# Token groups of 4, 8, 8, 8, 8, 8, 8 and 4 blocks in place of 6 and 8 in turn

## The chip, the cores and the metric

The kernel runs on one core of a Trainium2 chip. The metric is the device time of one execution in microseconds, the median of several runs. The core has a matrix engine (TensorE, PE in the profile, with its weight loads as PEld), VectorE (DVE), ScalarE (ACT), GpSimd (POOL) and SyncE (SP); POOL and SP also issue most of the transfers, each in the order of its own queue.

## What is computed

Attention with squared ReLU instead of softmax, for 8 batches of 12 heads, 448 positions and 64 columns each, and then a two-layer network over the 3584 tokens, with a sigmoid-approximated gelu between the layers:

```python
scores = scale * np.matmul(q, k.transpose(0, 1, 3, 2))
attn = np.maximum(scores, 0.0) ** 2 / S
attn_out = np.matmul(attn, v)
x = attn_out.transpose(0, 2, 1, 3).reshape(3584, 768)
h = x @ w_in                                # 768 -> 2048
g = h * (1.0 / (1.0 + np.exp(-1.702 * h)))
out = g @ w_out                             # 2048 -> 768
```

## The kernel before

**Attention.** The work is cut into 24 units: unit u is batch u // 3 and four of its twelve heads. A unit has 7 slots (key blocks of 64). For each slot four 64x64 score matmuls run side by side on TensorE (`scores`, L145), ACT or VectorE takes the ReLU out of PSUM (`relu2`, L159 and L156), VectorE squares (L430), and after the seventh slot 28 matmuls with v (`av_mm`, L174) give the unit's result, which `xt_evac` (L194, L197) copies to `xt`, the input of the first layer. The q and k of units 0 to 5 are loaded by POOL with a cast to 16 bits and transposed on TensorE (L129, L133); those of later units are loaded by SP (L82), cast by ACT (k) and POOL (q), and transposed by a transfer of SP (L111).

**Tokens.** A block is 64 tokens; 7 blocks make a batch, 56 the whole. The network works on groups of blocks, `gblk` (L41): 6, 8, 6, 8 and so on. A group's first layer needs all units that have a block of it. Two blocks are one tile of 128 tokens.

**First layer** (`m1`, L222): for each of 16 column blocks of `w_in`, six matmuls as wide as the group has tokens (384 or 512) into one of two PSUM banks (`ps_m`), then the gelu on ACT (L227, out buffer `gf`) and a scaling on POOL into `gt` (L229), the input of the second layer.

**Second layer.** Group 0 is done plainly (`m2`, L248): 2 x 16 matmuls of 384 columns for each tile. From group 1 on, two neighbouring tiles are done together by Strassen's scheme (`pair`, L287): seven products of 8 matmuls, 56 in place of 64, with sums of activations on VectorE (L282), sums of weights made once (`weight_sum`, L272, in quarters, called A to E), and evictions by ACT (L296) and VectorE (L298). A group of 6 blocks has three tiles: one pair, and one tile that has no partner (`single`), with two half products of 16 matmuls, 32 in all.

**Order.** The order of all instructions is written out as a string of words, and each engine takes its own part of it in that order. Words are: `s2.1` score slot 1 of unit 2 with its ReLU (`:d` on VectorE, `:t` scores issued twice, `:h` ReLU held back until after the next gelu or product), `x2.1` its square, `a2` the unit's matmuls with v and their copy to xt (`:m` in the two `ps_m` banks), `f0.3` column block 3 of group 0 in the first layer, `m` a plain half tile, `p1.0.4` product 4 of the pair that starts at tile 0 of group 1, `i` half a single. `jk`, `jq`, `jv` are POOL's loads of a unit's k, q, v, `jw` one of four blocks of w_in in two halves, `jo` one of four blocks of w_out; `k3` and `q3` are TensorE's transpositions; `G` a small copy that holds SP back until a block of w_out is there; `L`, `K`, `Q`, `R`, `W` loads, casts, transposition and v of later units; `z3` three matmuls of 512 zero columns into the buffer of the next scores. POOL's loads use eight semaphores in turn, so that each waits for the eighth before it.

Of the kernel before, what the change touches and what calls it, by code (L numbers as in the profile page):

```python
# [8 lines left out]
F32 = mybir.dt.float32  # L9
F16 = mybir.dt.float16  # L10
AF = mybir.ActivationFunctionType
ALU = mybir.AluOpType
# [3 lines left out]
def kernel(  # L16
# [9 lines left out]
    nc = tc.nc  # L26
    B, H, S, D = q.shape
# [10 lines left out]
    WO = 8  # L38


    gblk = [6, 8] * (B // 2)  # L41
    gcum = [0]
    for n in gblk:
        gcum.append(gcum[-1] + n)
# [14 lines left out]
    ps_s = ctx.enter_context(tc.tile_pool(name="ps_s", bufs=3, space=bass.MemoryType.PSUM))  # L59
    ps_m = ctx.enter_context(tc.tile_pool(name="ps_m", bufs=2, space=bass.MemoryType.PSUM))  # L60
# [74 lines left out]

    early = []

    def scores(u, j, times=1):
        st = units[u]
        sc = early.pop() if early else ps_s.tile([128, 2, 512], F32, name="sc", tag="sc")  # L140
        for s in [0, 1] * times:
            for a in range(2):
                r = slice(64 * a, 64 * a + 64)
                c = slice(64 * s, 64 * s + 64)
                nc.tensor.matmul(  # L145
                    out=sc[c, a, 0:S],
                    lhsT=st["kT"][r, j, c],
                    rhs=st["qT"][r, :, c],
                    start=True, stop=True)
        return sc  # L150

    def relu2(u, j, sc, dve=False):
        rl = rlp.tile([128, 2, S], F16, name="rl", tag="rl")
        at = atp.tile([128, 2, S], F16, name="at", tag="at")
        if dve:
            nc.vector.tensor_scalar(out=rl, in0=sc[:, :, 0:S], scalar1=0.0, scalar2=None,  # L156
                                    op0=ALU.max)
        else:
            nc.scalar.activation(out=rl, in_=sc[:, :, 0:S], func=AF.Relu)  # L159
        pend[u, j] = (at, rl)  # L160
        return at

# [43 lines left out]
    def release():  # L206
        while held:
            u, j, sc = held.pop()
            ats[u, j] = relu2(u, j, sc)
# [187 lines left out]
    with tc.manual_schedule():  # L397
# [21 lines left out]
                   "D": (w_d, wout[1][0], wout[0][0], ALU.add)}  # L419

        def slot(how, u, j):
            sc = scores(u, j, 2 if "t" in how else 1)
            if "h" in how:
                held.append((u, j, sc))
            else:
                ats[u, j] = relu2(u, j, sc, "d" in how)
# [13 lines left out]
        def zeros(how, n):  # L440
            early.append(ps_s.tile([128, 2, 512], F32, name="sc", tag="sc"))
            for _ in range(n):
                nc.tensor.matmul(out=early[0][:, 0, :], lhsT=zero[:, 0:128],
                                 rhs=zero[:, 0:512], start=True, stop=True)

        do = {"s": slot, "x": square, "z": zeros,
              "k": lambda how, u: trans_pe(u, "k"), "q": lambda how, u: trans_pe(u, "q"),
              "a": av,
# [20 lines left out]
            "f1.0 C0 m0.1.0 f1.1 K7 m0.0.0 s6.0:d s6.1 Q7 L8 s6.2 x6.0 A3 f1.2 f1.3 f1.4 f1.5 "
            "x6.2 s6.3 s6.4:h x6.1 E0 Q8 s6.5:d x6.3 x6.5 W6 R7 jo1.0 f1.6 A1 f1.7 s6.6 C3 s7.0 "  # L470
            "f1.8 x6.6 x6.4 K8 x7.0 f1.9 f1.10 L9 s7.1 Q9 R8 a6 L10 W7 s7.2 s7.3 E3 A2 f1.11 "
            "x7.1 C1 x7.2 K9 R9 x7.3 f1.12 s7.4:h s7.5 x7.5 m0.0.1 B3 B0 s7.6 B1 x7.6 x7.4 K10 "
            "Q10 s8.0 s8.1 x8.0 x8.1 f1.13 m0.1.1 A0 s8.2 x8.2 W8 a7 s8.3:d s8.4 L11 B2 m0.2.1 "
            "s8.5 x8.4 x8.3 s8.6 f1.14 D3 x8.5 x8.6 f1.15 W9 s9.0:d s9.1 x9.0 a8 R10 L12 s9.2 "
            "s9.3 p1.0.0 K11 f2.0 f2.1 C2 f2.2 x9.2 f2.3 x9.1 s9.4 s9.5:h x9.3 s9.6 p1.0.1 f2.4 "
            "D1 f2.5 f2.6 x9.4 E2 f2.7 s10.0 Q11 L13 x9.6 K12 s10.1:h s10.2:h x9.5 x10.0 f2.8 "
            "p1.0.2 x10.1 p1.0.3 Q12 x10.2 s10.3 a9 E1 x10.3 s10.4:d s10.5 f2.9 W10 f2.10 f2.11 "
            "R11 f2.12 p1.0.4 R12 x10.4 x10.5 s10.6 x10.6 s11.0 D0 s11.1 D2 f2.13 x11.0 W11 "
            "x11.1 p1.0.5 s11.2 a10 L14 s11.3:h s11.4 p1.0.6 x11.4 x11.2 Q13 K13 p1.2.0 f2.14 "
            "s11.5 x11.3 s11.6 f2.15 x11.5 p1.2.1 x11.6 L15 p1.2.2 s12.0 a11 s12.1 x12.0 "  # L480
            "s12.2:h p1.2.3 Q14 p1.2.4 s12.3 R13 x12.1 K15 s12.4:h K14 s12.5 x12.2 p1.2.5 "
            "p1.2.6 f3.0 f3.1 x12.5 x12.4 x12.3 s12.6:h s13.0:h s13.1 Q15 i2.2.1 R14 x13.1 "
            "i2.2.0 x13.0 L16 W12 p2.0.0 p2.0.1 s13.2:h L17 x12.6 a12 s13.3 f3.2 R15 f3.3 W13 "
            "x13.2 x13.3 f3.4 f3.5 p2.0.2 f3.6 s13.4 Q16 s13.5 s13.6 x13.4 f3.7 x13.5 W14 x13.6 "
            "f3.8 s14.0:d Q17 s14.1 x14.1 s14.2:h x14.0 K16 f3.9 W15 L18 p2.0.3 f3.10 x14.2 a13 "
            "s14.3 s14.4 f3.11 f3.12 x14.4 K18 x14.3 f3.13 K17 R16 f3.14 s14.5 s14.6 R17 "
            "s15.0:d x14.5 p2.0.4 x15.0 p2.0.5 x14.6 W16 W17 f3.15 s15.1:d a14 x15.1 s15.2:h "
            "s15.3 x15.3 p2.0.6 f4.0 s15.4:d x15.2 s15.5 s15.6:h p3.0.0 f4.1 f4.2 f4.3 x15.4 "
            "x15.5 Q18 L19 L20 x15.6 f4.4 s16.0:h s16.1:d s16.2 p3.0.1 x16.1 p3.0.2 x16.2 "
            "p3.0.3 K19 a15 s16.3:h s16.4 p3.0.4 p3.0.5 x16.0 R18 x16.4 p3.0.6 f4.5 Q19 W18 "  # L490
            "s16.5 s16.6 x16.5 s17.0:h x16.3 f4.6 p3.2.0 f4.7 x16.6 s17.1 s17.2:d x17.2 R19 "
            "x17.0 a16 x17.1 f4.8 p3.2.1 f4.9 p3.2.2 p3.2.3 f4.10 s17.3 s17.4 s17.5 p3.2.4 "
            "f4.11 x17.4 s17.6:h x17.3 W19 s18.0 x17.5 p3.2.5 x17.6 x18.0 p3.2.6 f4.12 L21 Q20 "
            "s18.1 K20 a17 s18.2 s18.3:h x18.1 f4.13 f4.14 L22 x18.2 f4.15 s18.4:d x18.4 "
            "s18.5:h f5.0 i4.2.1 Q21 x18.3 s18.6 x18.5 W20 s19.0:d x19.0 s19.1 x18.6 R20 i4.2.0 "
            "f5.1 f5.2 x19.1 p4.0.0 s19.2 a18 Q22 s19.3:h s19.4 f5.3 f5.4 K22 f5.5 p4.0.1 K21 "
            "x19.2 x19.3 f5.6 x19.4 f5.7 p4.0.2 s19.5 s19.6 L23 s20.0 p4.0.3 f5.8 x19.5 x19.6 "
            "f5.9 p4.0.4 Q23 x20.0 s20.1 s20.2 R21 x20.1 x20.2 a19 s20.3:h s20.4 f5.10 p4.0.5 "
            "p4.0.6 K23 x20.3 s20.5 x20.4 s20.6 s21.0 f5.11 x20.5 x20.6 R22 f5.12 s21.1:d s21.2 "
            "x21.1 x21.0 a20 s21.3:d s21.4 f5.13 x21.4 x21.2 x21.3 f5.14 f5.15 p5.0.0 s21.5 W21 "  # L500
            "x21.5 s21.6 s22.0:h f6.0 x21.6 p5.0.1 f6.1 p5.0.2 p5.0.3 x22.0 s22.1 a21 s22.2 "
            "s22.3 x22.3 f6.2 f6.3 x22.2 R23 f6.4 f6.5 p5.0.4 f6.6 x22.1 W22 f6.7 s22.4 s22.5:d "
            "s22.6 x22.5 p5.0.5 p5.0.6 p5.2.0 x22.6 f6.8 x22.4 s23.0:d x23.0 s23.1:h p5.2.1 "
            "p5.2.2 s23.2 s23.3 x23.1 a22 x23.2 s23.4 f6.9 f6.10 W23 f6.11 f6.12 x23.3 f6.13 "
# [40 lines left out]
```

## Time and profile before

| | |
|---|---|
| median of 5 runs | 382.64 us (382.53 to 384.86) |
| the profiled execution | 383.17 us, of which the span from first to last instruction is 381.4 us |
| granted clock of TensorE | 0.998 |
| first layer, matmuls of 512 columns | 384, 379 ns each from issue to end |
| first layer, matmuls of 384 columns | 384, 326 ns each from issue to end |
| ReLU on ACT | 144, 917 ns |
| square on VectorE | 168, 664 ns |
| gelu on ACT, 512 and 384 columns | 64 each, 599 and 493 ns |

Matmuls overlap: the time from one start to the next is shorter than the duration in the table. The page's second part cuts the span into 40 slices of 9.5 us; a digit is the busy share in tenths:

```profile
PE   7789999999999999999999999999999999999994
DVE  3999763778958886556788875638777865313374
ACT  2887763796776758367664656476764461232210
POOL 7555552753254323056340424332142231222200
DMA  8999999799946595789872809541730423101133
```

TensorE is full from the fourth slice to the last but one; VectorE and the DMA engines are full in the first slices; ACT, VectorE and POOL are lightly loaded in the last six, where attention is over.

### The profile page before, as it was taken

How to read it: one execution, taken by the hardware profiler on the slowest of the kernel's cores; microseconds unless marked ns; L12 is line 12 of the kernel's file. 1: busy time of each engine (PE TensorE's matmuls, PEld its weight loads, DVE VectorE, ACT ScalarE, POOL GpSimd, SP SyncE). 2: the span in 40 equal slices, each digit the busy share in tenths (PEclk: the TensorE clock that was granted, in tenths of full speed). 3: DMA queues.
4: the chain of work that ended last, by engine and by line, in shares of the span. 5: the costliest groups of instructions: out<-in, count | busy, mean ns of one | idle time of the engine just before them, and what ended most of it. 6: DMA issues, size and time to landing. Idle time of an engine off the chain costs nothing.

```text
span 381.4 us, 7864 instructions
## 1 busy us (share of the span) xinstructions
PE 369.5 (97%) x3136; PEld 192.8 (51%) x3136; DVE 256.6 (67%) x425; ACT 214.6 (56%) x314; POOL 136.2 (36%) x200
## 2 busy tenths in 40 slices
PE   7789999999999999999999999999999999999994
PEld 3355555445455555544555555544455555455552
DVE  3999763778958886556788875638777865313374
ACT  2887763796776758367664656476764461232210
POOL 7555552753254323056340424332142231222200
PEclk9999999999999999999999999999999999999999
DMA  8999999799946595789872809541730423101133
GB/s 120 169 190 205 205 265 220 149 193 185 252 143 144 87 288 132 189 143 177 143 209 76 168 7 300 109 128 22 142 62 0 108 26 83 43 0 41 43 83 83
DMA packets 65221, 50.85 MB, mean 133 GB/s; under 512 B 35744, under 2 KB 61728, under 8 KB 65184
## 3 DMA queue, kind: packets, MB, share of 16 engines
q1 hardware_dynamic: 47872, 35.70, 38.7%
q0 software_dynamic: 17152, 14.55, 26.4%
q8 instruction: 24, 0.39, 0.4%
q10 hardware_dynamic: 160, 0.10, 0.1%
q14 instruction: 13, 0.11, 0.1%
HBM read 45.61 MB, written 11.01 MB: 148 GB/s over the span
## 4 chain that ended last, share of the span: by engine, by line
PE 89%; DVE 5%; DMA 3%; issue 2%; ACT 1%; POOL 0%; ACTq 0%; POOLq 0%
PE ht L222 39%; PE op L287 29%; PE sc L145 9%; PE av L174 7%; PE op L248 4%; DMA k<-in_k_dram 3%; DVE at L430 2%; DVE osb L298 1%; PE tr L129 1%; DVE xt L197 1%; DVE kT L133 0%; DVE qT L133 0%; ACT eb L296 0%; ACT rl L159 0%; DVE as L282 0%
## 5 line engine op out<-in xcount | busy, mean ns | idle before, releaser
L222 PE MATMUL ht<-xt,win 128*128 128x384 f16 (+1 forms) x768 | 156.2, 353 | 0.4 <-ACT gf L227 0.4
L229 POOL TENSOR_SCALAR gt<-gf 128x384 f16<-128x384 f32 (+1 forms) x128 | 82.5, 645 | 200.2 <-ACT gf L227 197.8
L159 ACT ACTIVATE rl<-sc 128x896 f16<-128x896 f32 x144 | 126.2, 917 | 42.9 <-PE sc L145 35.5
L227 ACT ACTIVATE gf<-ht 128x384 f32<-128x384 f32 (+1 forms) x128 | 69.6, 546 | 85.3 <-PE ht L222 75.8
L430 DVE TENSOR_TENSOR at<-rl 128x896 f16<-128x896 f16 x168 | 105.9, 664 | 13.6 <-ACT rl L159 13.0
L222 PEld LDWEIGHTS <-win 128*128 128x128 f16 x768 | 72.4, 98 | 74.9 <-issue 12.0
L287 PEld LDWEIGHTS <-gt 128*128 128x128 f16 x408 | 38.6, 98 | 30.1 <-issue 3.8
L145 PE MATMUL sc<-qT,kT 64*64 64x448 f16 x696 | 48.6, 357 | 1.1 <-ACT rl L159 0.7
L287 PEld LDWEIGHTS <-as 128*128 128x128 f16 x312 | 29.9, 98 | 22.9 <-issue 2.9
L287 PE MATMUL op<-wsum,gt 128*128 128x384 f16 x224 | 40.6, 326 | 0.0
L287 PE MATMUL op<-wout,as 128*128 128x384 f16 x224 | 40.0, 326 | 0.0
L298 DVE SCALAR_TENSOR_TENSOR osb<-op,osb 128x384 f32<-128x384 f32 (+1 forms) x45 | 23.6, 544 | 23.6 <-PE op L287 23.3
L156 DVE TENSOR_SCALAR rl<-sc 128x896 f16<-128x896 f32 x24 | 26.1, 1087 | 16.2 <-PE sc L145 15.8
L174 PE MATMUL av<-at,v 64*64 64x448 f16 x616 | 33.2, 350 | 0.2 <-DVE at L430 0.2
L287 PE MATMUL op<-wout,gt 128*128 128x384 f16 (+1 forms) x184 | 32.4, 319 | 0.5 <-DVE osb L298 0.5
L194 DVE CAST xt<-av 128x896 f16<-128x896 f32 (+2 forms) x32 | 24.5, 792 | 11.6 <-PE av L174 11.6
L298 DVE SCALAR_TENSOR_TENSOR osb<-op,ea 128x384 f32<-128x384 f32 x22 | 12.1, 552 | 27.8 <-PE op L287 12.2
L145 PEld LDWEIGHTS <-kT 64*64 64x64 f16 x696 | 17.2, 105 | 24.8 <-issue 17.2
L174 PEld LDWEIGHTS <-v 64*64 64x64 f16 x672 | 19.7, 107 | 12.8 <-issue 2.7
L282 DVE TENSOR_TENSOR as<-gt 128x1024 f16<-128x1024 f16 x36 | 24.5, 706 | 0.7 <-POOL gt L229 0.7
L104 POOL CAST q<-qst 128x896 f16<-128x896 f32 x18 | 17.5, 971 | 8.0 <-issue 4.7
L91 POOL DMA_DIRECT2D v<-in_v_dram x24 | 18.0, 750 | 4.5 <-DMA win<-in_moe_w_in_dram 2.9
(38 smaller groups left out, 168.9 us busy)
## 6 DMA issues: line engine op xcount, KB each, us to landing
out_dram<-osb SPq DMA_DIRECT2D x54, 192.0 KB, 2.9
kst<-in_k_dram SPq DMA_DIRECT2D x18, 448.0 KB, 5.9
qst<-in_q_dram SPq DMA_DIRECT2D x18, 448.0 KB, 6.5
v<-in_v_dram POOLq DMA_DIRECT2D x24, 224.0 KB, 5.2
win<-in_moe_w_in_dram POOLq DMA_DIRECT2D x8, 384.0 KB, 11.3
wout<-in_moe_w_out_dram POOLq DMA_DIRECT2D x4, 768.0 KB, 12.5
q<-in_q_dram POOLq DMA_DIRECT2D x6, 224.0 KB, 7.0
k<-in_k_dram POOLq DMA_DIRECT2D x6, 224.0 KB, 5.3
```

What stands on the lines that cost most here:

```text
L145: nc.tensor.matmul(out=sc[c, a, 0:S], lhsT=st["kT"][r, j, c], rhs=st["qT"][r, :, c], start=True, stop=True)
L156: nc.vector.tensor_scalar(out=rl, in0=sc[:, :, 0:S], scalar1=0.0, scalar2=None, op0=ALU.max)
L159: nc.scalar.activation(out=rl, in_=sc[:, :, 0:S], func=AF.Relu)
L174: nc.tensor.matmul(out=st["av"][s][64 * a:64 * a + 64, 0:S], lhsT=st["v16"][r, a, 64 * j:64 * j + 64], rhs=at[r, a, :], start=(j == 0), st ...
L194: nc.vector.tensor_copy(out=xts[g][:, 2 * pr:2 * pr + 2, c], in_=st["pair"][:, :, f])
L222: nc.tensor.matmul(out=ht[:, 0:n], lhsT=w[:, kk, fo:fo + 128], rhs=xts[g][:, kk, 0:n], start=(kk == 0), stop=(kk == NK - 1))
L227: nc.scalar.activation(out=gf[:, 0:n], in_=ht[:, 0:n], func=AF.Gelu_apprx_sigmoid, scale=1.0 / SC)
L229: nc.gpsimd.tensor_scalar(out=gts[g][:, f, 0:n], in0=gf[:, 0:n], scalar1=SC, scalar2=1.0, op0=ALU.mult, op1=ALU.mult)
L282: nc.vector.tensor_tensor(out=out_, in0=x, in1=y, op=op)
L287: nc.tensor.matmul(out=op[:, 0:cw], lhsT=lhs[:, f, :], rhs=w[:, f, c0:c0 + cw], start=(start and f == 0), stop=(stop and f == HF - 1))
L298: nc.vector.scalar_tensor_tensor(out=o, in0=op[:, 0:w], scalar=sc, in1=add, op0=ALU.mult, op1=ALU.add)
L430: nc.vector.tensor_tensor(out=at, in0=rl, in1=rl, op=ALU.mult)
```

## The change

The groups become 4, six times 8, and 4 blocks. Group 0, still done plainly, has two tiles; every later group has two or four, so that `single` is no longer called. A score slot gets an option `m`, to put its scores in the two `ps_m` banks, and the ReLU code can then take the two banks one by one. The string of words is replaced as a whole; its beginning is shown up to the unit that completes the second batch, and further on only the places where groups begin.

```diff
-    gblk = [6, 8] * (B // 2)
+    gblk = [4, 8, 8, 8, 8, 8, 8, 4]
...
-    def scores(u, j, times=1):
+    def scores(u, j, times=1, banks=False):
         st = units[u]
-        sc = early.pop() if early else ps_s.tile([128, 2, 512], F32, name="sc", tag="sc")
+        if early:
+            sc = early.pop()
+        elif banks:
+            sc = [ps_m.tile([128, 512], F32, name="scm", tag="mm") for _ in range(2)]
+        else:
+            sc = ps_s.tile([128, 2, 512], F32, name="sc", tag="sc")
...
-        if dve:
-            nc.vector.tensor_scalar(out=rl, in0=sc[:, :, 0:S], scalar1=0.0, scalar2=None,
-                                    op0=ALU.max)
-        else:
-            nc.scalar.activation(out=rl, in_=sc[:, :, 0:S], func=AF.Relu)
+        halves = [(rl, sc[:, :, 0:S])] if not isinstance(sc, list) else [
+            (rl[:, a, :], sc[a][:, 0:S]) for a in range(2)]
+        for o, i in halves:
+            if dve:
+                nc.vector.tensor_scalar(out=o, in0=i, scalar1=0.0, scalar2=None, op0=ALU.max)
+            else:
+                nc.scalar.activation(out=o, in_=i, func=AF.Relu)
...
-            sc = scores(u, j, 2 if "t" in how else 1)
+            sc = scores(u, j, 2 if "t" in how else 1, "m" in how)
...
-            "jq0 jk0 I q0 k0 z3 s0.0:d x0.0 s0.1 x0.1 jq1 jk1 s0.2 q1 s0.3 x0.2 x0.3 s0.4 k1 "
-            "x0.4 z3 jk4 jk2 s0.5 s0.6 k2 k4 x0.5 s1.0 s1.1 jv0 x0.6 s1.2 jq3 x1.0 x1.1 a0:m "
-            "s1.3 s1.4 x1.2 jq2 s1.5 jk3 q2 jk5 x1.3 x1.4 jv2 s1.6 x1.5 jv1 k3 s2.0:t q3 x1.6 "
-            "jw0 s2.1:t x2.1 s2.2:t x2.0 s2.3:t x2.2 a1:m x2.3 s2.4:t jq4 jq5 s2.5:t s2.6 x2.4 "
-            "x2.5 x2.6 jv3 jw1 jv4 k5 s3.0 jv5 a2 s3.1 q4 jw2 x3.0 x3.1 s3.2 f0.0 q5 x3.2 jw3 "
-            "s3.3:d s3.4 x3.3 s3.5 x3.4 jo0.1 f0.1 f0.2 s3.6 s4.0:d x3.5 s4.1 f0.3 f0.4 x4.0 G1 "
-            "x3.6 a3 x4.1 s4.2 x4.2 jo0.0 s4.3 x4.3 f0.5 L6 f0.6 s4.4 s4.5:h x4.4 s4.6:d f0.7 "
-            "f0.8 L7 f0.9 x4.6 f0.10 x4.5 s5.0:d x5.0 s5.1 a4 s5.2 s5.3 f0.11 x5.2 f0.12 jo1.1 "
-            "x5.1 x5.3 s5.4 s5.5:d x5.4 s5.6 f0.13 f0.14 x5.5 f0.15 K6 Q6 x5.6 R6 a5 m0.2.0 "
-            "f1.0 C0 m0.1.0 f1.1 K7 m0.0.0 s6.0:d s6.1 Q7 L8 s6.2 x6.0 A3 f1.2 f1.3 f1.4 f1.5 "
...
+            "jk0 jq0 I k0 q0 s0.0:d jq1 s0.1 x0.0 q1 x0.1 jk1 s0.2 s0.3 x0.2 jq2 s0.4 jq4 k1 z3 "
+            "s0.5 jv0 x0.3 jv3 s1.0 jv1 x0.4 jk2 x0.5 jk3 s1.1 jk4 x1.0 q2 jq3 jv5 x1.1 s0.6 "
+            "x0.6 jq5 q4 s1.2 a0 s1.3 jw0 s1.4 x1.2 k2 jv2 x1.3 s1.5 x1.4 s1.6 x1.5 x1.6 k3 "
+            "s2.0:t a1 x2.0 s2.1:t s2.2:t q3 x2.1 jw1 x2.2 s2.3:t x2.3 s3.0 s2.4:t x3.0 jv4 "
+            "s2.5:t s2.6 q5 x2.4 jw2 x2.5 x2.6 s3.1 s3.2 x3.1 a2:m x3.2 s3.3 jk5 s3.4 x3.4 f0.0 "
+            "s3.5:h k4 x3.3 s3.6 x3.6 jo0.1 f0.1 f0.2 f0.3 x3.5 jw3 s4.0 a3 s4.1 x4.0 s4.2 f0.4 "
+            "f0.5 s4.3 x4.1 x4.2 s4.4 G1 s4.5:h k5 x4.3 f0.6 z3 f0.7 f0.8 x4.4 s4.6 x4.5 s5.0:d "
+            "jo0.0 L6 f0.9 x4.6 s5.1 s5.2 x5.0 x5.1 f0.10 s5.3 x5.2 a4 s5.4 f0.11 s5.5 x5.3 "
+            "s5.6 f0.12 x5.4 K6 L7 f0.13 x5.5 x5.6 a5 f0.14 Q6 f0.15 f1.0 f1.1 f1.2 jo1.1 f1.3 "
+            "C0 R6 C3 L8 m0.1.0 C2 jo1.0 f1.4 Q7 s6.0 Q8 K8 s6.1 x6.0 s6.2:h f1.5 K7 x6.1 W6 "
+            "m0.0.0 s6.3 s6.4 f1.6 x6.2 R7 E3 f1.7 L9 f1.8 R8 A2 x6.3 s6.5:d s6.6 x6.5 B1 f1.9 "
+            "x6.4 x6.6 B3 m0.0.1 A3 s7.0 A1 x7.0 s7.1 f1.10 x7.1 s7.2 Q9 s7.3:d a6 x7.2 K9 "
...
+            "x23.4 p5.0.0 s23.5 s23.6 x23.5 p5.0.1 x23.6 p5.0.2 a23 p5.0.3 p5.0.4 f6.0 p5.0.5 "
+            "p5.0.6 f6.1 f6.2 f6.3 p5.2.0 p5.2.1 f6.4 f6.5 f6.6 f6.7 f6.8 p5.2.2 f6.9 p5.2.3 "
+            "p5.2.4 f6.10 p5.2.5 f6.11 f6.12 p5.2.6 f6.13 f6.14 f6.15 p6.0.0 f7.0 f7.1 f7.2 "
+            "f7.3 p6.0.1 f7.4 f7.5 f7.6 f7.7 p6.0.2 p6.0.3 p6.0.4 p6.0.5 p6.0.6 p6.2.0 f7.8 "
+            "f7.9 f7.10 f7.11 f7.12 p6.2.1 p6.2.2 p6.2.3 p6.2.4 p6.2.5 p6.2.6 f7.13 f7.14 f7.15 "
+            "p7.0.0 p7.0.1 p7.0.2 p7.0.3 p7.0.4 p7.0.5 p7.0.6").split()
```

The first group that waits for a batch late in the string: before, f4.0 comes after a14, f5.0 after a17 and f6.0 after a20; after, f4.0 comes after a17, f5.0 after a20 and f6.0 after a23.

## The prediction

> **What bounds the kernel now.** I read the page's totals first, then the chain of waits in order of time, then the busy time by stretches, then single lines of the timeline and single tiles' landings in the stretch where the chain is not TensorE.
>
> ```profile
> span 381.4 us, 7864 instructions
> PE 369.5 (97%) x3136; PEld 192.8 (51%) x3136; DVE 256.6 (67%) x425; ACT 214.6 (56%) x314; POOL 136.2 (36%) x200
> PE 89%; DVE 5%; DMA 3%; issue 2%; ACT 1%; POOL 0%; ACTq 0%; POOLq 0%
> ```
>
> The chain is TensorE for 89% of the span. Where it is, and at what pace, its pieces tell (start us, us, what):
>
> ```profile
> 28.50 0.51 PE tr L129 x14
> 29.32 1.08 PE ht L222 x6
> 30.41 0.51 PE tr L129 x14
> 30.92 0.69 PE sc L145 x12
> ...
> 54.52 2.71 PE op L248 x16
> 57.22 1.29 PE ht L222 x6
> 58.52 2.60 PE op L248 x16
> ...
> 193.53 3.90 PE ht L222 x24
> ...
> 347.96 7.77 PE ht L222 x36
> ```
>
> From 29.3 us, the first product of the first layer (word f0.0), TensorE issues without a hole to the end stage; before that the pieces are DMA, VectorE and short bursts. So the time is: when f0.0 can start, plus all that TensorE has still to issue, plus the little that stalls. The paces: a 384-column matmul takes 3.90/24 = 0.1625 us, a 512-column one 7.77/36 = 0.216, three score slots 0.69 (0.23 each), one transposition of k or q about 0.51, and the first matmul group after a 64x64 stretch costs 0.11 more (2.71 against 2.60 for the same 16).
>
> ```profile
> 0.00:29.00 29.00, 23.17 (x374) 12.51 (x374) 21.62 (x43) 19.73 (x24) 17.75 (x30) 1.00 1.06 160
> 29.00:54.00 25.00, 25.00 (x268) 13.16 (x270) 20.53 (x32) 19.41 (x31) 13.77 (x22) 1.00 1.21 220
> ```
>
> Columns: stretch, length, busy us of PE, PEld, DVE, ACT, POOL, clock, DMA share, GB/s. Up to 54 us the DMA engines are saturated and ACT and DVE are some 80% busy; TensorE is full only from 29 us.
>
> **What the Trainium skill says.** "TensorE: Matmul & The Clock Gate", section "Back-to-back issue gap", gives N/2.4 + 2.5 ns: 162.5 ns for 384 columns and 215.8 for 512, which is what the chain shows; its other figure there, 131 ns for 512 in a real stream, is not what this trace has. For 256 columns, which no row shows, I estimate 109 ns from the formula. "ScalarE: Activation LUTs", section "Rules for kernel authors", has 0.83 ns an element beside a fixed part; the gelus here take 493 ns for 384 and 599 for 512, the same slope, so 0.39 us for 256 is estimated. "DMA: Bandwidth & Descriptors", section "Issuing engines are not separate DMA queues", says that transfers of all issuing engines interleave on the same 16 DMA engines; the share of 1.21 above agrees that nothing is gained there by another order, only exchanged.
>
> **The change part by part.**
>
> Second layer. Before: group 0 is 3 tiles of 32 matmuls (96); 11 pairs of 7 products of 8 (616); 3 singles of 32 (96): 808. After: 2 plain tiles (64) and 13 pairs (728): 792. Sixteen fewer at 0.1625: -2.6 us. All are on TensorE, and with them the three singles' sums and evictions go from VectorE, which waits anyway.
>
> First layer. 768 matmuls both times; columns before 384 x 0.1625 + 384 x 0.216 = 145.3 us, after 576 x 0.216 + 192 x 0.109 = 145.3: nothing. Weight loads (98 ns each, overlapped) fit under 109 ns. What I can't see is whether a 256-column run waits for its bank: two banks give 2 x 0.655 = 1.31 us, and filling, draining, gelu and semaphores add up to about 1.36 (0.55 to issue six, 0.27 for the last one to end by the first page's section "Single matmul latency", (398 + N)/2.4 ns, which gives the 326 and 379 ns that the rows show for 384 and 512, 0.39 for the gelu, and 0.10 and 0.05 between them as the timeline has it for 512 columns). So up to 0.05 for a group in a run; the last 16 groups come in runs: 0.0 to 0.6, taken 0.2.
>
> The start. This is where I see the price. The load of unit 2's v (jv2) moves in POOL's queue from place 12 to place 18, behind both halves of the first w_in block (jw0) and behind loads of units 3 to 5. Before (POOL's timeline, the landing of the q at 17.5 us, and VectorE's timeline, whose four squares end with x2.6 and whose casts write xt after a2):
>
> ```profile
> 15.47 0.72 POOL L91 DMA_DIRECT2D v<-in_v_dram  x1
> 16.18 1.36 POOL L383 DMA_DIRECT2D win<-in_moe_w_in_dram  x2
> 17.50 0.75 POOL L119 DMA_DIRECT2D q<-in_q_dram  x1
> DMA to landing us min/median/max: 10.6/10.6/10.6
> 25.59 2.28 DVE L430 TENSOR_TENSOR at<-rl 128x896 f16<-128x896 f16 x4
> 28.36 1.16 DVE L194 CAST xt<-av 128x768 f16<-128x768 f32 x2
> ```
>
> The q at 17.5 us, place 16, lands 10.6 later, at 28.1, with 13 small loads and the two halves ahead of it. In the new order v2 has 15 small ones ahead: two more at 1.1 us (consecutive small loads land that far apart) less about 1 us in which the queue ran dry because POOL waited for a transposition at 11 to 14 us, which the new order does not do there: v2 lands at about 29.3 (28.3 to 31). Then a2's 28 matmuls (1.35), the drain and two casts of 256 columns (0.9): f0.0 at 31.6 against 29.3, +2.3 (1.3 to 4). ACT and VectorE don't undercut it: one more relu and square (s3.0) and one more cast stand before a2's inputs, so these are ready at about 28.9 instead of 27.9.
>
> What TensorE has left from f0.0: two slots fewer (26 against 24 are done by then), -0.5; transpositions of k4 and k5 instead of q5 alone, +0.6; one of the two runs of three 512-column zeros (z3) moves from before the first scores to between f0.6 and f0.7, where TensorE is full, 3 x 0.216 = +0.65; three more changes between 64x64 and 128x128, +0.3.
>
> Less cover before a5. Group 1 can't start before unit 5 is done. Between f0.0 and the end of a5 TensorE now has 14 groups of 0.655, 16 slots, three avs of 1.35, two transpositions, the zeros and the changes, about 19.7 us, against 25 before. ACT in that time has 15 relus (two in a row take 1.73, so 0.82 each) and 11 gelus of 0.3 to 0.4: 16 us. It fits, with some interleaving lost: 0 to 1, taken 0.4. The filling from f0 is thinner, and the work that group 0 gives up (two blocks of tokens) comes after a5, in groups 1 to 7: it is already in the totals.
>
> End stage. After a23 there are 32 products and 32 groups against 21 products, one half single and 16 groups. ACT, VectorE and POOL are far under half busy there. A pair whose products follow without a group between loses 0.23 us, as the kernel before shows at 363.6 (a wait for VectorE's eviction); three such pairs against two: +0.2. The last pair and its stores are the same.
>
> Middle. For units 6 to 23 all PE words are the same in kind and number of switches (46 and 47). f4, f5 and f6 start one unit's batch later relative to attention; each waits for its a word (a17, a20, a23) long before, or under two products. SP's order puts L10 behind the stores of m0.1.1, due about 10 us before K10 needs it, landing takes 6: hidden. The option "m" of the score slots is used by no word, so the bank edits cost and bring nothing.
>
> Sum: -2.6 - 0.5 + 0.6 + 0.65 + 0.3 + 2.3 + 0.4 + 0.2 + 0.2 = +1.55. The profiled execution took 383.2 (span 381.4 and 1.8 around it); the median of the five runs is 382.64, 0.5 below. The change applies to both: 384.1.
>
> **Rivals.**
>
> The saving arrives whole: v2 is early, the start is as before and zeros and transpositions fall into holes: 382.64 - 2.6 = 380.0. For it: TensorE is the chain, and 16 matmuls are really gone. Against it: the place of jv2 behind jw0, in a queue whose landings are in order of issue.
>
> Late w_out (slower). The last quarter of w_out (jo1.0) is issued by POOL after the gelu of f1.3, at about 59 us, and is needed by VectorE's sum B1, and by m0.0.1 on TensorE, at about 72. Squares x6.4 and x6.6 are queued behind B1 on VectorE, and behind these a6. The four w_out loads before took:
>
> ```profile
> DMA to landing us min/median/max: 4.0/11.9/15.1
> ```
>
> (the 4.0 is the gate's small copy; the four are 9.1 to 15.1). Above 13 us each microsecond is TensorE's, since group 1 is all it has: up to 2.2, 386.3. For it: L8, L9 and three units' transpositions run at the same time. Against it: w_in and the first half of w_out land earlier than before.
>
> Start later still: v2 after 31 us, or ACT a slot behind all the way to a5; each microsecond counts fully: 385.5 to 387.
>
> **How the numbers follow.** Forecast (about +1.5) 0.50; whole saving 0.08; late w_out 0.24; later start 0.18. What a measurement can tell from no change is about 0.5%, 380.7 to 384.6: faster 0.08, same 0.50, slower 0.42. The forecast's unknowns (start -1.0/+1.7, bank runs and interleaving -0.6/+1) give 382.4 to 386; the late cases take the upper end to 387, and the lower goes to 381.8.
>
> **What would show it.** Right: f0.0 near 31.6 with a2 waiting for v; a5's end near 51.5 instead of 54.5; 792 second-layer matmuls; matmuls of 256 columns at 109 ns. Wrong: f0.0 at 30 or before (then the time is under 383), a hole on TensorE around 72 us behind wsum or wout, or holes in the middle from relus or squares that a fixed order placed too tightly, of which before has hardly any.

## The result, and the profile after

| | before | after |
|---|---|---|
| median | 382.60 us (382.18 to 385.61, 47 runs) | 385.04 us (383.67 to 388.81, 28 runs) |
| after to before | | 1.0059, 95% interval 1.0047 to 1.0072 |
| the profiled execution | 383.17 us, span 381.4 | 384.92 us, span 383.1 |

The change costs 2.4 us by the medians and 1.75 us by the two profiled executions. The page's totals and the chain by engine, after:

```profile
span 383.1 us, 7873 instructions
...
PE 369.3 (96%) x3120; PEld 192.1 (50%) x3120; DVE 262.7 (69%) x441; ACT 217.6 (57%) x321; POOL 133.7 (35%) x200
...
PE 88%; DMA 5%; DVE 2%; issue 2%; POOL 1%; ACT 1%; ACTq 0%
```

The sixteen matmuls are gone (x3120 against x3136), but TensorE's busy time is the same within 0.2 us. VectorE and ACT have a little more, and the DMA part of the chain has grown from 3% to 5%. Where that is, the chain in order of time says (start us, us, what):

```profile
10.09 7.32 DMA k<-in_k_dram
17.69 10.34 DMA v<-in_v_dram
52.78 6.00 PE ht L229 x30
58.78 2.60 PE op L255 x16
...
339.41 2.74 PE ht L229 x24
```

The load of v2 is on the chain: issued at 17.69, landed at 28.03, where before nothing waited for it. The stretch of full TensorE begins later, and the piece at 52.78 is preceded by a hole. The last line is a run of the new 256-column matmuls: 2.74/24 = 0.114 us each, a little above the 0.109 of six in a row. TensorE's timeline after (start us, us, engine, line, operation, tiles, count, and in brackets the idle time before it and what ended it):

```profile
28.08 1.52 PE L181 MATMUL avm<-at,v 64*64 64x448 f16 x28 [0.88 <-DMA v<-in_v_dram]
29.43 0.55 PE L150 MATMUL sc<-qT,kT 64*64 64x448 f16 x8
30.80 0.82 PE L229 MATMUL ht<-xt,win 128*128 128x256 f16 x6 [0.82 <-DVE xt L204]
...
50.82 0.83 PE L229 MATMUL ht<-xt,win 128*128 128x256 f16 x6
52.78 6.00 PE L229 MATMUL ht<-xt,win 128*128 128x256 f16 x30 [1.13 <-ACT gf L234]
```

and the same place in the kernel before:

```profile
27.93 0.38 PE L174 MATMUL av<-at,v 64*64 64x448 f16 x4 [0.21 <-DVE at L430]
28.11 0.38 PE L145 MATMUL sc<-qT,kT 64*64 64x448 f16 x4
28.43 0.58 PE L129 MATMUL tr<-ident,q 128*64 128x128 f16 x14
28.94 0.38 PE L145 MATMUL sc<-qT,kT 64*64 64x448 f16 x4
29.26 1.15 PE L222 MATMUL ht<-xt,win 128*128 128x384 f16 x6
```

Before, a2 waits for the last square alone, and VectorE's casts hide behind a transposition and two slots; f0.0 comes at 29.26. After, a2 waits for v, then f0.0 for the casts, and comes at 30.80: 1.54 later. The hole at 52.78 names a gelu; why that gelu is late stands on ACT's timeline:

```profile
49.30 0.40 ACT L234 ACTIVATE gf<-ht 128x256 f32<-128x256 f32 x1
51.51 0.95 ACT L102 ACTIVATE k<-kst 128x896 f16<-128x896 f32 x1 [1.80 <-DMA kst<-in_k_dram]
52.37 0.64 ACT L234 ACTIVATE gf<-ht 128x256 f32<-128x256 f32 x2
```

ACT stands 1.80 us at the word K6, the cast of unit 6's k, whose load landed at 51.41. The gelu of f0.13 is queued behind it, and TensorE needs that gelu's bank. In the kernel before K6 comes after the gelu of f0.15, and ACT's 0.49 us there held nobody.

This hole belongs to some executions and not to all. The kernel of "Sixteen more" below has the order of the changed kernel, and the same matmuls up to group 2; in its trace the k of unit 6 landed at 47.16, and K6 waits for nothing:

```profile
49.57 0.97 ACT L102 ACTIVATE k<-kst 128x896 f16<-128x896 f32 x1
```

That execution took 386.29 us; without its sixteen matmuls (2.61, see there) 383.7 would be left, an estimate, and the shortest of the changed kernel's 28 times is 383.67. How many of the 28 had the hole is not shown. In five traces with K6 at this place the load landed at 47.2 to 48.6 where SP issued it ahead of POOL's load of w_out[0][0], and at 51.4 and 52.4 where SP came second. That is a pattern and not a test; with K6 late it landed at 52.3 although SP came first.

**A ledger of TensorE.** From the trace I took the start of each matmul to the start of the next, from the first of f0.0 to the last of the kernel, and summed by class. The sum is then exact, waits included (each wait counts to the class ahead of it):

| us | before | after | difference |
|---|---|---|---|
| first layer, 768 matmuls | 149.60 | 151.57 | +1.97 |
| second layer, 16 fewer | 134.68 | 131.84 | -2.84 |
| scores, 144 and 142 slots | 33.84 | 33.95 | +0.11 |
| products with v, 588 | 28.23 | 28.08 | -0.15 |
| transpositions, 14 and 28 | 0.51 | 1.03 | +0.52 |
| zeros, none and 3 | 0 | 0.65 | +0.65 |
| sum, before rounding | 346.88 | 347.12 | +0.24 |

The second layer did save, and the rest gave it back. Inside the first layer, 33 changes from it to 64x64 work or to a transposition have become 38, at 0.09 us each beyond the plain pace (+0.46); the hole at K6 is 1.29 by this count, start to start and beyond the pace (1.13 of it with the engine idle); the last group, 96 matmuls of 256 columns, takes 11.36 us where 96 x 0.1092 is 10.48 (+0.88); and a wait of the kernel before at 121.77 us, 0.53 beyond the pace, is not there. These four make +2.10, and smaller waits take back 0.13. In the second layer 16 x 0.1625 is 2.60, and three changes to 64x64 work fewer (17 in place of 20) are 0.28.

### The profile page after: what moved, and what is told of

The parts are those of the page before. It is cut to its first block, busy times and chain, and to the rows that moved or that the text cites. A ratio compares the mean times of both kernels' runs of the same rounds, so it can differ in the third digit from the quotient of the medians.

```text
span 383.1 us, 7873 instructions
## 1 busy us (share of the span) xinstructions
PE 369.3 (96%) x3120; PEld 192.1 (50%) x3120; DVE 262.7 (69%) x441; ACT 217.6 (57%) x321; POOL 133.7 (35%) x200
## 4 chain that ended last, share of the span: by engine, by line
PE 88%; DMA 5%; DVE 2%; issue 2%; POOL 1%; ACT 1%; ACTq 0%
PE ht L229 39%; PE op L294 29%; PE sc L150 9%; PE av L181 7%; PE op L255 3%; DMA v<-in_v_dram 3%; DMA k<-in_k_dram 2%; DVE osb L305 2%; PE zp L412 1%; PE tr L129 1%; POOL v L91 1%; PE avm L181 0%; ACT gf L234 0%; DVE xt L204 0%; ACT eb L303 0%
## 5 line engine op out<-in xcount | busy, mean ns | idle before, releaser
L229 PE MATMUL ht<-xt,win 128*128 128x512 f16 (+1 forms) x768 | 157.9, 353 | 2.1 <-ACT gf L234 1.3
L236 POOL TENSOR_SCALAR gt<-gf 128x512 f16<-128x512 f32 (+1 forms) x128 | 80.3, 628 | 216.5 <-ACT gf L234 215.3
L166 ACT ACTIVATE rl<-sc 128x896 f16<-128x896 f32 x147 | 128.8, 921 | 29.8 <-PE sc L150 26.9
L234 ACT ACTIVATE gf<-ht 128x512 f32<-128x512 f32 (+1 forms) x128 | 69.5, 547 | 97.3 <-PE ht L229 81.7
L437 DVE TENSOR_TENSOR at<-rl 128x896 f16<-128x896 f16 x168 | 106.2, 662 | 14.7 <-ACT rl L166 13.9
L305 DVE SCALAR_TENSOR_TENSOR osb<-op,osb 128x384 f32<-128x384 f32 (+1 forms) x53 | 27.8, 544 | 19.5 <-PE op L294 19.3
L294 PE MATMUL op<-wout,gt 128*128 128x384 f16 (+1 forms) x216 | 38.3, 320 | 0.5 <-DVE osb L305 0.5
L294 PE MATMUL op<-wsum,gt 128*128 128x384 f16 x208 | 37.5, 326 | 0.0
L201 DVE CAST xt<-av 128x640 f16<-128x640 f32 (+6 forms) x40 | 26.1, 688 | 8.6 <-PE av L181 8.5
L164 DVE TENSOR_SCALAR rl<-sc 128x896 f16<-128x896 f32 x21 | 22.6, 1085 | 8.7 <-PE sc L150 8.6
L305 DVE SCALAR_TENSOR_TENSOR osb<-op,eb 128x384 f32<-128x384 f32 x26 | 14.3, 549 | 7.5 <-PE op L294 7.5
```

The costliest lines, as they stand in the source:

```text
L164: nc.vector.tensor_scalar(out=o, in0=i, scalar1=0.0, scalar2=None, op0=ALU.max)
L166: nc.scalar.activation(out=o, in_=i, func=AF.Relu)
L201: nc.vector.tensor_copy(out=xts[g][:, 2 * pr:2 * pr + 2, c], in_=st["pair"][:, :, f])
L229: nc.tensor.matmul(out=ht[:, 0:n], lhsT=w[:, kk, fo:fo + 128], rhs=xts[g][:, kk, 0:n], start=(kk == 0), stop=(kk == NK - 1))
L234: nc.scalar.activation(out=gf[:, 0:n], in_=ht[:, 0:n], func=AF.Gelu_apprx_sigmoid, scale=1.0 / SC)
L236: nc.gpsimd.tensor_scalar(out=gts[g][:, f, 0:n], in0=gf[:, 0:n], scalar1=SC, scalar2=1.0, op0=ALU.mult, op1=ALU.mult)
```

## The experiments

The kernels are compared with the changed kernel (385.04) or with the kernel before by ratio, each with runs of the kernel before on the same chip. These had medians of 382.35 to 382.71 from chip to chip, so a difference of 0.3 us between two series says little. A trace shows one execution, which can be a microsecond off its kernel's median.

**v2 early.** Does the late v2 explain the loss?

```diff
-            "... s1.3 jw0 s1.4 x1.2 k2 jv2 x1.3 ..."
+            "... s1.3 jv2 jw0 s1.4 x1.2 k2 x1.3 ..."
```

> The changed kernel with one word moved: unit 2's v (jv2) is issued before the first block of w_in (jw0), not after it. In the changed kernel's trace a2 waits 0.88 us for this v and f0.0 starts at 30.80. Theory (the places in the first stretch add up one by one): f0.0 at about 30.2, time 0.6 us less. Rival (one hole takes it back): ACT waits 1.80 us at K6 for the k of unit 6, which lands at 51.41 whatever ACT does; what comes earlier ahead of it only waits longer there, so f0.0 is earlier by 0.6 and the time is the same within 0.3.

384.91 us (6 runs), ratio to before 1.0063 (1.0039 to 1.0087): no gain to be seen, the rival's time. v landed at 24.6 and a2 did not wait for it, but f0.0 came at 30.25, only 0.55 earlier, and this, on TensorE and on ACT, followed:

```profile
39.07 0.58 PE L129 MATMUL tr<-ident,k 128*64 128x128 f16 x14 [0.63 <-DMA k<-in_k_dram]
...
53.77 3.40 PE L229 MATMUL ht<-xt,win 128*128 128x256 f16 x18 [1.96 <-ACT gf L234]
```

```profile
52.49 0.95 ACT L102 ACTIVATE k<-kst 128x896 f16<-128x896 f32 x1 [2.63 <-DMA kst<-in_k_dram]
```

What the start gained was lost at 39.07, where unit 5's k is awaited; in the changed kernel nothing waits there. ACT then came to K6 no earlier (49.86 against 49.71), and unit 6's k was issued 1.3 later and landed at 52.39 in place of 51.41, so the hole has grown from 1.13 to 1.96. So this is not the rival's mechanism, a fixed landing that eats an earlier arrival. The profiled execution took 385.94, 1.0 above the median of its kernel, and does not stand for all. The late v2 is a cost of the change, but taking it away alone showed no gain.

**Zeros back.** The second run of three zero matmuls returns ahead of the first scores.

```diff
-            "jk0 jq0 I k0 q0 s0.0:d ..." / "... f0.6 z3 f0.7 ..."
+            "jk0 jq0 I k0 q0 z3 s0.0:d ..." / "... f0.6 f0.7 ..."
```

> The changed kernel with the second run of three zero matmuls back ahead of the first scores, out of the stretch between f0.6 and f0.7. If TensorE's issue time is what counts there: 0.65 us less. Rival, as for the v: the wait at K6 grows by what is saved ahead of it, 0.0 to 0.2 less. A third possibility: ACT sets the pace between f0.0 and a5 and the zeros were in a hole; then also nothing, but with K6 late too (the run with all three) nothing as well.

385.57 us (6 runs), 1.0080 (1.0063 to 1.0097): a miss. In five of the six runs the mean granted clock of TensorE was 0.989 to 0.993, which is taken up below. The trace is of the sixth (0.996), which took 384.40 us, 0.5 less than the profiled execution of the changed kernel. In it v landed later, at 29.2, and a2 waited longer:

```profile
29.22 1.52 PE L181 MATMUL avm<-at,v 64*64 64x448 f16 x28 [1.98 <-DMA v<-in_v_dram]
```

f0.0 came 1.15 later than in the changed kernel, but from there on the ledger is 1.66 shorter: the zeros' 0.65, and 1.01 in the first layer, where the hole at K6 is missing (the k of unit 6 landed at 48.63). What the zeros cost was measured later in a cleaner place.

**K6 late.** K6 goes behind the gelu of f0.15, where the kernel before has it.

```diff
-            "... x5.4 K6 L7 f0.13 x5.5 x5.6 a5 f0.14 Q6 f0.15 f1.0 ..."
+            "... x5.4 L7 f0.13 x5.5 x5.6 a5 f0.14 Q6 f0.15 K6 f1.0 ..."
```

> The changed kernel with ACT's cast of unit 6's k (K6) moved behind the gelu of f0.15. TensorE's hole of 1.13 us before f0.15, which ends with ACT's gelu, should go: 1.0 to 1.2 us less, if unit 6's transposed k, two us later, is still there for s6.0 (62 us). If the loss lies in the middle or end of the kernel instead, the hole moves to s6.0 or to w_out and the time stays.

384.35 us (6 runs), 1.0057 (1.0035 to 1.0078), some 0.7 less than the changed kernel by the medians, but by the ratio (1.0059 there) not to be told from it. In the trace, of an execution of 386.00 us, the hole at K6 is gone, and the next one stands where group 1's first column blocks end:

```profile
57.65 1.24 PE L229 MATMUL ht<-xt,win 128*128 128x512 f16 x5
59.67 1.62 PE L255 MATMUL op<-wout,gt 128*128 128x384 f16 x9 [0.78 <-ACT gf L234]
```

The releaser named is a gelu, but the gelu whose bank this matmul takes had ended at 58.29; w_out[0][0], which it reads, landed at 59.53.

**All three.**

> The changed kernel with all three: v early, zeros back, K6 late. If the three prices are real and only hidden by the wait at K6: 0.6 + 0.65 + 1.1 = 2.35 us less than the changed kernel, within 0.2% of the kernel before. If the block of w_out that lands at 56.8 us or the last one at 70.9 becomes the next wait, only 1.1 to 1.7 less, with a hole of TensorE behind wout or wsum near 57 or 70 us.

383.64 us (19 runs: 18 of 382.45 to 384.39, and one, the profiled one, of 1824.81 us, unexplained), 1.0020 (1.0007 to 1.0032) without that one: 1.4 us below the changed kernel, the size that the rival gave, and more than the three alone together seemed to give (0.1, none, 0.7, none of them clear of the spread). In the one trace of each single edit some other wait is there or has grown; that it is so in every execution is not shown. The same kernel once more, for its trace:

> The kernel with v early, zeros back and K6 late again, for its trace. Theory: a2 without a wait for v, f0.0 at 30.2 or before, no wait at K6, and a hole of 0.8 to 2 us before m0.1.0, ended by the landing of the first half of w_out. Rival: TensorE full from f0.0 on, and the time in the middle.

It took 383.41 us. No hole of TensorE behind a transfer is left after f0.0, at w_out neither, so the rival's wait is not there; and a2 doesn't wait for v. Still f0.0 is at 30.68. TensorE's and VectorE's timelines at that place:

```profile
27.57 1.79 PE L181 MATMUL avm<-at,v 64*64 64x448 f16 x28
29.17 0.57 PE L150 MATMUL sc<-qT,kT 64*64 64x448 f16 x8
30.68 0.81 PE L229 MATMUL ht<-xt,win 128*128 128x256 f16 x6 [0.94 <-DVE xt L204]
```

```profile
26.70 0.62 DVE L133 COPY qT<-tr 128x896 f16<-128x896 f16 x1 [0.33 <-PE tr L129]
27.24 2.37 DVE L437 TENSOR_TENSOR at<-rl 128x896 f16<-128x896 f16 x4
29.52 1.28 DVE L204 CAST xt<-avm 128x256 f16<-128x256 f32 x4
```

VectorE copies q5's transposition (0.62) and squares slot 3.0 ahead of the last squares of unit 2, and then casts a2's result in four pieces (1.28) where the form with one buffer takes two. So a second cause of the late start was hidden under v2: VectorE's own order.

**An earlier w_out[0][0].** All three, with that load straight behind jw3 and SP's gate on it.

```diff
-            "... x3.5 jw3 s4.0 ... G1 s4.5:h ... s5.0:d jo0.0 L6 ..."
+            "... x3.5 jw3 jo0.0 s4.0 ... G0 s4.5:h ... s5.0:d L6 ..."
```

> The changed kernel with v early, zeros back and K6 late, and besides the half of w_out that m0.1.0 needs (jo0.0) issued right after the last block of w_in (behind jw3) instead of after s5.0, with SP's gate waiting for that half, so that unit 6's and 7's loads by SP no longer share the DMA engines with it. Theory (what the faster order lost it lost to transfers of the first 60 us: v2 at a2, kst at K6, w_out at m0.1.0): no hole of TensorE over 0.5 us after f0.0 until the end stage; by the sum of the prediction without these waits, 382.6 - 2.6 - 0.5 + 0.6 + 0.3 + 0.4 + about 0.9 for f0.0 = 381.7, faster than the kernel before by 0.2 to 0.3%. Rival (the DMA engines are full up to 60 us, so any order only moves the hole): a new hole of 1 us or more at K6, at s6.0 or at f0.12, and 383 to 384.

386.33 us (6 runs), 1.0098 (1.0069 to 1.0127): 2.7 us slower than all three. The rival's mechanism held, a new hole at K6, and the time is 2.3 us above its range. With the gate on the later load, kst6 was issued at 50.52 instead of about 43 and landed at 54.40:

```profile
54.50 0.95 ACT L102 ACTIVATE k<-kst 128x896 f16<-128x896 f32 x1 [2.81 <-DMA kst<-in_k_dram]
```

**Sixteen more.** To see what a second-layer matmul is worth, the first product of the pairs in groups 2 and 4 is issued twice into the same bank.

```diff
             product(A[0][0], w_b, op)
+            if m == 0 and g in (2, 4):
+                product(A[0][0], w_b, op)
```

> The changed kernel with product 0 of the first pairs of groups 2 and 4 issued twice, 16 matmuls of 384 columns more, on TensorE in the middle, as many as the change took away; the result is the same. If TensorE bounds the middle: +2.6 us. If something else paces it there: less than 1.5.

387.58 us (4 runs), 1.0137 (1.0098 to 1.0175): 2.5 above the changed kernel. Four runs are few, two of them have a mean clock of 0.989 and 0.992, and the profiled execution (386.29) is 1.3 below the median, without the hole at K6; the ledger is the better measure. In it the second layer grew from 131.84 to 134.45, by 2.61. The saving of the change is real and worth what it was priced at.

**The kernel before with v2 later**, behind jw0 as in the changed kernel.

```diff
-            "... x1.3 x1.4 jv2 s1.6 x1.5 jv1 k3 s2.0:t q3 x1.6 jw0 s2.1:t ..."
+            "... x1.3 x1.4 s1.6 x1.5 jv1 k3 s2.0:t q3 x1.6 jw0 jv2 s2.1:t ..."
```

> The kernel before with one word moved: unit 2's v (jv2) is issued behind the first block of w_in (jw0), as the changed kernel has it, at place 15 instead of 12. Theory: v lands at about 28, a2 waits 1 to 1.5 us for it, f0.0 moves from 29.3 to 30.3 to 30.8 and the time rises by 1.0 to 1.5 us, since this kernel has no later hole to take it up; in some executions TensorE, idle before a2, is granted half its clock for some 3.4 us as in one trace of the changed kernel, and these are a further microsecond longer. Rival: f0.0 is set by ACT and VectorE there and the time stays within 0.4.

382.62 us (22 runs), 1.0005 (0.9989 to 1.0020): nothing, and my expectation was a miss. v landed at 25.4, a2 did not wait, f0.0 came at 28.56. In this kernel the place behind jw0 is the 15th in POOL's queue, not the 18th, with 12 small loads and the two halves ahead. With 15 small loads and no half ahead (v2 early) v landed at 24.6. Neither alone makes v2 late for a2; the two together do (28.03). The run has another use: from f0.0 to the end it has the same ledger as the kernel before (346.98 against 346.88) and f0.0 is 0.7 earlier, with a time at the median. So I infer that the profiled execution of the kernel before had a late start, and that its median belongs to a start of about 28.6; there is no second trace of that kernel.

**a2's inputs first.** All three, and on VectorE a2 comes ahead of x3.0 and q5, in one buffer instead of the two banks.

```diff
-            "... x2.3 s3.0 s2.4:t x3.0 jv4 s2.5:t s2.6 q5 x2.4 jw2 x2.5 x2.6 s3.1 s3.2 x3.1 a2:m x3.2 s3.3 jk5 s3.4 x3.4 f0.0 s3.5:h ..."
+            "... x2.3 s2.4:t jv4 s2.5:t s2.6 x2.4 jw2 x2.5 x2.6 s3.0 a2 s3.1 x3.0 jk5 s3.2 x3.1 f0.0 q5 x3.2 s3.3 s3.4 x3.4 s3.5:h ..."
```

> All three edits of the earlier run (v2 issued before jw0, zeros back before s0.0, K6 behind f0.15), and the inputs of a2 ahead on VectorE: a2 comes before x3.0 and the cast of q5, and no longer in the banks ps_m that make it wait for tile 3's slots. Theory (what is left of the start's 1.3 us is VectorE's order: the square sums of block 2 end after casts that a2 doesn't need): a2 ends near 27.9, f0.0 at 29.2 to 29.6 in place of 30.7, first plain second-layer matmul near 55.7, time 382.2 to 382.8. Rival (the next transfer takes it back): w_out[0][0], which lands near 55.8, or kst6 holds TensorE, a wait behind gf or wout of 0.5 to 1.5 us at 54 to 57 us, time 383.3 to 384.

383.37 us (22 runs), 1.0030 (1.0015 to 1.0044): not to be told from all three. f0.0 came at 28.35, earlier than expected, 2.33 before all three's. Of that, 0.97 is work that now stands behind it (q5's transposition 0.51, two slots 0.46, by the ledger); most of the true gain of 1.4 went into this:

```profile
28.35 0.82 PE L229 MATMUL ht<-xt,win 128*128 128x256 f16 x6
...
33.02 1.25 PE L229 MATMUL ht<-xt,win 128*128 128x256 f16 x10 [0.86 <-DVE kT L133]
```

f0.2 waits for the bank of k4's transposition, whose copy VectorE makes after a square that itself waits for ACT. The rival's time was right, its place wrong: not a transfer this time.

**Zeros in the wait.** Zeros back, with five more zero matmuls just ahead of a2; what they compute is not used.

```diff
-            "... s3.1 s3.2 x3.1 a2:m ..."
+            "... s3.1 s3.2 x3.1 z5 a2:m ..."
```

> The zeros-back kernel with five more zero matmuls just before a2, so that TensorE has work while a2's v is on its way. They compute nothing that is used. Theory (the half-clock stretch at 28 us comes from the idle wait for v): mean granted clock 0.995 or more in all runs, time 383.9 to 384.5, against 385.57 for zeros back alone, with v landing no earlier. Rival (the stretch has another cause, the thin work before it): clocks of 0.989 to 0.993 remain in most runs and the time is 385 or more.

384.44 us (8 runs), 1.0045 (1.0021 to 1.0070): five matmuls more, and 1.1 us less than zeros back alone. The clock was 0.997 to 1.000 in all eight runs. v landed at 28.5 in this trace, and the zeros held a2 until 29.31, no earlier than without them (29.22):

```profile
28.14 1.24 PE L450 MATMUL sc<-zero 128*128 128x512 f16 x5 [0.43 <-ACT rl L166]
29.31 1.52 PE L181 MATMUL avm<-at,v 64*64 64x448 f16 x28
```

With work in the wait none of eight runs has a low clock, without it five of six (on another chip). So the idle wait for v has a second price, the clock that follows it.

**The zeros' price.** In the kernel before, the second three zero matmuls go from behind x0.4 to behind f0.6.

```diff
-            "... s0.4 k1 x0.4 z3 jk4 ..." / "... L6 f0.6 s4.4 ..."
+            "... s0.4 k1 x0.4 jk4 ..." / "... L6 f0.6 z3 s4.4 ..."
```

> The kernel before, with its second group of three zero matmuls moved from behind x0.4 to between f0.6 and s4.4, where the changed kernel has it in effect (beside a bound TensorE). Theory (my step: in a stretch without holes three matmuls of 216 ns cost their whole time): +0.65, 383.2 to 383.4. Rival (they fall into a wait of the stretch and cost nothing): 382.5 to 382.8.

383.16 us (22 runs), 1.0021 (1.0006 to 1.0036): +0.61 over its 382.55, as priced. In the ledger 347.54 against 346.88. The profiled execution took 384.58: its f0.0 came at 30.05, behind a half-clock stretch at 13.9 us, which is taken up below.

**k4 ahead.** a2 first, with the next wait taken away and a transposition put into a hole.

```diff
-            "... x2.5 x2.6 s3.0 a2 ... s3.5:h k4 x3.3 ... C0 R6 C3 L8 m0.1.0 C2 jo1.0 f1.4 Q7 ..."
+            "... x2.5 x2.6 k4 s3.0 a2 ... s3.5:h x3.3 ... R6 L8 jo1.0 f1.4 C0 C3 m0.1.0 C2 Q7 ..."
```

> The kernel with a2's inputs first, and k4's transposition moved from behind f0.0 into TensorE's wait for ScalarE ahead of a2 (0.4 us at 25.2 and at 26.1 there), and m0.1.0 and its weight sums C0, C3 behind f1.4, so that w_out[0][0] (landed 56.42) has landed when they come. Theory (0.58 us of transposition goes into a hole, and the 0.86 us hole at 33 us, where f waits for the copy of k4's transposition, goes): f0.0 at 28.3 to 28.6, no hole at 33 us, 1.2 to 1.4 us less than a2 first: 382.0 to 382.3, ratio to before 0.9985 to 1.0. Rival (a transfer or VectorE takes it back again, as twice before): a hole of over 0.5 us between 30 and 71 us and 382.6 to 383.4.

382.92 us (14 runs), 1.0011 (0.9997 to 1.0025): 2.1 us below the changed kernel and not to be told from the kernel before. The time lies in the rival's range, and so does the sign: a hole of over 0.5 us at 31 us. The transposition costs nothing now, f0.0 comes at 28.22, and a wait for ACT's ReLU took the place of the other:

```profile
24.71 0.58 PE L129 MATMUL tr<-ident,k 128*64 128x128 f16 x14
...
28.22 0.85 PE L229 MATMUL ht<-xt,win 128*128 128x256 f16 x6
...
31.01 0.38 PE L150 MATMUL sc<-qT,kT 64*64 64x448 f16 x4 [0.70 <-ACT rl L166]
```

No version here beats the kernel before. In this one's ledger the second layer has 131.93, 2.75 less than before; the first layer 150.79 (+1.19), the scores 35.44 (+1.60, of it 0.94 idle in two waits), the transpositions 1.02 (+0.51).

## Why the prediction was right and wrong

The range held the time (385.04 in 381.8 to 387.0), the sign was right, and the likeliest time, 384.1, was 0.9 too low. The ratio lies just past the half per cent that I called no change, a case to which I gave 0.42 against 0.50. (The sum itself is 382.64 + 1.55 = 384.2, not 384.1.)

By the two profiled executions the change is +1.75 where the sum said +1.55. That is in part luck. The start was put 0.8 too dear, and a wait of the kernel before, 0.53, was not seen to go; against that stand 1.29 at K6, which was not foreseen, and 0.7 in the last group. Smaller differences make up the rest.

- *Second layer, -2.6*: -2.84 in the ledger, 2.60 of it the matmuls and the rest changes of form, and 2.61 for sixteen by the sixteen-more run. Right. VectorE did not lose work with the singles, as I had it: it has 6.1 us more (262.7 against 256.6), since two pairs more bring sums and evictions of their own.
- *The start, +2.3 (1.3 to 4)*: the mechanism was right, v2 behind 15 small loads and two halves. It landed at 28.03, not 29.3, earlier than my bounds (28.3 to 31); in the zeros-back trace it landed at 29.2. f0.0 was 1.54 later by the two traces, and about 2.2 later if the kernel before has a start of 28.6 at its median, as inferred. I had VectorE's order in the text ("don't undercut it"), but as something hidden under v2. The v2-early run shows that it is a limit of its own: f0.0 at 30.25, 1.0 us behind the traced start of the kernel before, with no wait for v.
- *Two slots -0.5, transpositions +0.6, zeros +0.65*: -0.47 by two slots of 0.23, with the class of scores +0.11 as a whole, because it also has the changes of form; +0.52; +0.65, and +0.61 by its own run. Right.
- *Three more changes of form, +0.3*: five more out of the first layer, +0.46, and three fewer out of the second, -0.28: two more in all. About right.
- *Less cover before a5, +0.4 (0 to 1)*: here a step is missing. I compared ACT's busy time (16 us) with TensorE's (19.7) and saw that it fits, and it did: from f0.0 to the end of a5 TensorE has no hole, it took 20.1 us, as forecast (19.7 + 0.4), and a5 ended at 50.89, earlier than the 51.5 forecast. I did not ask what K6, which had moved from behind f0.15 to before f0.13, waits for, and put nothing for it. Its load does not come earlier with it; in the profiled execution ACT stood 1.80 us and TensorE 1.13 just behind a5, in the v2-early one TensorE 1.96, and in three traces with K6 at the same place nothing. K6 stands where a late landing holds TensorE; how often that happens is open.
- *256-column runs, +0.2 (0.0 to 0.6)*: the pace of 0.109 was right, the wait for the bank was not: +0.88 in the last group, a term mis-sized. Of it 0.8 falls between one column block and the next, most of it not in the turn of the two banks that I had estimated (last section).
- *End stage, +0.2*: right. The wait of 0.23 in a pair stands three times, against two before; from the start of the last matmul to the end of the span it is 5.2 in both. That the wait of the kernel before at 121.77 us would go (0.53) I had not counted.
- *"The change applies to both"*: the sum was set on a profiled execution 0.5 above the median. By the medians the prediction is 0.9 off. If the profiled start of the kernel before was late, as inferred, it could not be carried over.

The rival of a late w_out did not happen: the last quarter landed at 70.91, without a wait at 72. Only when K6 was moved did a w_out load hold TensorE, and it was another one, w_out[0][0]. The rival of the whole saving fell with the start; the later start (v2 after 31) did not come in any trace.

What is shown: the saving's worth, the zeros' price, that VectorE's order holds the start once v2 is early (a2 first), and that the order of the first 60 us is worth 2.1 us, which brings the change back to the kernel before. Not shown apart is how much of the median belongs to the late v2, to K6 and to the clock. For the clock there is a hint of the size: the 22 of the changed kernel's 28 runs with a mean clock above 0.993 have a median of 384.6, 0.4 below that of all. What holds the last group is read from the trace and was not tried by itself.

## What to carry to other kernels

A matmul taken away from a TensorE that bounds the kernel was worth its full pace here, where TensorE runs without holes; price the start and the thin stretch behind it separately, and there ask of each word that moved ahead when its transfer lands, not only whether its engine has time. Where several waits end within a microsecond of each other, removing one can show nothing, as here: remove them together, and read in the trace which is next. Look for a wait in a second trace of the same order before you blame the order for it. And compare a profiled execution with the median before adding to it, since a late start in that one execution goes straight into the sum.

## What had not been expected of the hardware

**A half-clock stretch after a half-idle wait.** Two traces caught it inside the kernel. The first is that of K6 late. Stretches of 3.4 us (length, busy us of PE, PEld, DVE, ACT, POOL with counts, TensorE's clock, DMA share, GB/s):

```profile
21.50:24.90 3.40, 2.90 (x58) 1.41 (x51) 3.40 (x8) 3.02 (x4) 1.98 (x3) 1.00 1.25 207
24.90:28.30 3.40, 1.84 (x34) 0.88 (x33) 3.07 (x6) 3.40 (x5) 0.71 (x1) 1.00 1.24 204
28.30:31.70 3.40, 3.40 (x36) 1.39 (x34) 1.51 (x5) 1.32 (x3) 0.00 (x0) 0.50 1.25 205
31.70:35.10 3.40, 2.95 (x41) 2.11 (x39) 2.90 (x7) 2.63 (x5) 1.47 (x2) 1.00 1.24 206
```

```profile
28.19 2.78 PE L181 MATMUL avm<-at,v 64*64 64x448 f16 x28 [0.88 <-DMA v<-in_v_dram]
```

For one stretch the clock is 0.50, and a2's 28 matmuls take 2.78 us in place of 1.52. "TensorE: Matmul & The Clock Gate" of the Trainium skill, in "What's actually happening", says that the clock is halved after an idle window of about 3.4 us, counted in windows that run on by themselves. The length agrees; but the window before was not idle, TensorE was busy for 1.84 of its 3.40 us. The second trace is that of the zeros' price, where three zero matmuls have been taken out just ahead of a wait of 1.50 us for a k; the stretch before it and the one at half clock:

```profile
10.50:13.90 3.40, 1.62 (x42) 1.01 (x38) 3.02 (x7) 3.18 (x4) 0.73 (x2) 1.00 1.06 138
13.90:17.30 3.40, 3.40 (x46) 1.65 (x44) 3.30 (x6) 2.44 (x3) 3.22 (x5) 0.50 1.21 185
```

Counted back in steps of 3.41 us from the clock's change at the end of each trace, a stretch busy for 1.80 in the kernel before (11.5 to 14.9) and one busy for 1.90 in zeros back (27.8 to 31.2) have full clock behind them. So the border lies near half here, and these traces don't fix it. That the windows run by themselves fits that only some executions have such a dip. Over 383 us it takes 0.004 off the mean clock: of the four kernels with a2 waiting for v (the changed one, zeros back, K6 late, sixteen more) 14 of 44 runs had a mean clock of 0.993 or less; of the other experiments' 119 runs 3, and of 114 runs of the kernel before beside them 2. In the changed kernel these are 6 of 28, with a mean of 386.2 us. The mean is a blunt sign: the two traced executions with the dip have 0.994 and 0.995 and are not among these.

**A pace that is right can still be too short.** Six matmuls of 256 columns need 0.655 us, and the sixteen blocks of the last group took 0.71 on average (11.36/16). The turn of two banks is the smaller part: I had estimated it at 0.05 too long for two blocks, and inside the runs it shows as 0.04 at every second block, start to start. Most of the 0.88 lies in five single waits. Four, of 0.09 to 0.16, come before the second block behind a product of the second layer, which each time starts 0.05 to 0.06 us after ACT or VectorE has emptied that product's bank. The fifth is 0.32, at 356.45, behind a gelu that started late; ACT's lines for one of the four (which ends at 339.94; the block starts at 339.99) and for the fifth:

```profile
339.45 0.49 ACT L303 ACTIVATE ea<-op 128x384 f32<-128x384 f32 x1 [0.64 <-PE op L294]
...
356.01 0.76 ACT L234 ACTIVATE gf<-ht 128x256 f32<-128x256 f32 x2 [0.63 <-POOL gt L236]
```
